# A fixed, woven instruction order with one-bank PSUM tiles in an attention, Fourier and FFN kernel

## The chip, the core and the metric

The kernel runs on one core of a Trainium2 chip. The metric is the device time in microseconds (us), as the median of several timed executions. The span that a profile shows is that of one profiled execution, 1 to 3 us shorter than the timed ones. Five engines matter: TensorE (PE; PEld is its weight load), VectorE (DVE), ScalarE (ACT), GpSimd (POOL) and SyncE (SP; SPq is its queue, which issues most transfers).

## The reference

For each of 8 batches, 512 rows of `x` attend to a 32-row state, and the state attends to the rows, in 8 heads of 64. The 544 rows that come out go through a real Fourier mix over rows and columns, a normalisation and a two-layer FFN. Cut to what matters:

```python
scores = x @ state.T / 8;  xread = softmax(scores) @ state     # 512 rows of each head
scores2 = state @ x.T / 8; sread = softmax(scores2) @ x        # 32 rows of each head
x = concat([xread, sread])                  # (8, 544, 512) after the heads are joined
u = x + real(fft(fft(x, axis=1), axis=2))
un = (u - mean(u)) / sqrt(var(u) + 1e-6)
out = u + relu(un @ w_ch1) @ w_ch2          # 512 -> 2048 -> 512
```

## The kernel before

One function, `front(b)`, does attention and transform of a batch; `ffn` does the two layers. The order of instructions on each engine was left to a scheduler. Every PSUM tile outside of the FFN is a pair of banks, of which there are two buffers.

```python
psQ = ctx.enter_context(tc.tile_pool(name="psQ", bufs=2, space=bass.MemoryType.PSUM))
psF = ctx.enter_context(tc.tile_pool(name="psF", bufs=2, space=bass.MemoryType.PSUM))
# ... x of batch 0, then the weights, which share the DMA engines with it
load_x(0)
for q in range(4):
    nc.gpsimd.dma_start(out=w1[:, :, q * 512:(q + 1) * 512], in_=w1v[:, :, q * 512:(q + 1) * 512])
# ... cut: w2, state, sine and cosine tables
def q2(name, dt=F32):
    return psQ.tile([128, 2, 512 if dt == F32 else 1024], dt, name=name, tag="q")
# ... in front(b): the state's reads (srp), copied into row block 0 of XR head by head
srp = q2("srp")
for g in range(2):
    for si in range(4):
        nc.tensor.matmul(srp[:, g, 0:257], lhsT=E[:, si, g, :], rhs=xin[:, si, 257 * g:257 * g + 257], ...)
rcs = wk.tile([128, 2], F32, name="rcs", tag="rcs")
nc.vector.reciprocal(rcs, srp.rearrange("p g c -> p (g c)")[:, 0:769:768])
# ... for g in 2, hh in 4: eight small rows, all on VectorE
nc.vector.tensor_scalar(XR[0:32, 0, c0:c0 - 64:-1], in0=srp[ph, g, ...], scalar1=rcs[ph, g:g + 1], ...)
# ... in ffn, for each of the four output tiles of a batch
nc.vector.scalar_tensor_tensor(ot, in0=po, scalar=rstd, in1=u, op0=ALU.mult, op1=ALU.add)
for d in dst:
    if isinstance(d[0], slice):                      # straight rows, and the "low" rows: 1 or 31 rows each
        nc.sync.dma_start(out=d[1], in_=ot[d[0], :])
        continue
    b, k = d                                         # reversed rows: out to DRAM, and from there to their place
    nc.sync.dma_start(out=r_dram[b, k], in_=ot)
    nc.sync.dma_start(out=out[b, top:top - 128:-1, :].rearrange("r (c n) -> c r n", c=2),
                      in_=r_dram[b, k].rearrange("r (c n) -> c r n", c=2))
# ... the main loop
ready = [front(0)]
for b in range(B):
    ready.append(front(b + 1))                       # while it exists
    ffn(*ready[b])
    if b % 4 == 3:
        ffn(*front_low(b // 4))
```

The softmax here doesn't subtract the row's maximum and nothing guards it: scores larger than these inputs give would overflow.

Of the kernel before, what the change touches and what calls it, by code (L numbers as in the profile page):

```python
# [12 lines left out]
F32 = mybir.dt.float32  # L13
BF16 = mybir.dt.bfloat16
# [14 lines left out]
def kernel(  # L29
# [24 lines left out]
    psQ = ctx.enter_context(tc.tile_pool(name="psQ", bufs=2, space=bass.MemoryType.PSUM))  # L54
    psF = ctx.enter_context(tc.tile_pool(name="psF", bufs=2, space=bass.MemoryType.PSUM))

# [7 lines left out]
    li = singles.tile([128, dm], I32, name="li")  # L64
    lt = singles.tile([128, NM], I32, name="lt")
    nc.gpsimd.iota(pi_[:, 0:2], pattern=[[128, 2]], base=1, channel_multiplier=1)
    nc.gpsimd.iota(pi_[:, 3:5], pattern=[[128, 2]], base=0, channel_multiplier=1)
    for hh in range(4):
# [10 lines left out]
    nc.sync.dma_start(  # L79
        out=stf.rearrange("p b g d -> p (b g) d"),  # L80
        in_=state.rearrange("b (g hh) j d -> (hh j) (b g) d", hh=4),
    )
    xin_bufs = []
    for i in range(2):
        t = singles.tile([128, 4, 514], BF16, name=f"xin{i}")
        xin_bufs.append(t)

    def load_x(b):
        xs = wk.tile([128, 4, dm], F32, name="xs", tag="xs")
        xb = x[b].rearrange("h s d -> s h d")  # L90
        for ps, si, rows in (
            (slice(0, 128), 0, xb[1:129]),
            (slice(0, 128), 1, xb[129:257]),
            (slice(0, 128), 2, xb[256:384]),
            (slice(0, 128), 3, xb[384:512]),
            (slice(0, 1), 2, xb[0:1]),
        ):
            nc.sync.dma_start(out=xs[ps, si, :].rearrange("p (h d) -> p h d", d=D), in_=rows)
        t = xin_bufs[b % 2]
        if b == 0:  # L100
            for si in range(4):
                if si % 2 == 0:
                    nc.vector.tensor_copy(t[:, si, 1:513], xs[:, si, :])  # L103
                else:
                    nc.scalar.copy(t[:, si, 1:513], xs[:, si, :])
        else:
            nc.gpsimd.tensor_copy(t[:, :, 1:513], xs)  # L107

    for i in range(2):
        nc.vector.memset(xin_bufs[i][:, :, 0:514:513], 1.0)  # L110
    load_x(0)
# [4 lines left out]
    for q in range(4):  # L116
        nc.gpsimd.dma_start(out=w1[:, :, q * 512:(q + 1) * 512], in_=w1v[:, :, q * 512:(q + 1) * 512])
    for q in range(2):
        nc.gpsimd.dma_start(out=w2[:, q * 8:(q + 1) * 8, :], in_=w2v[:, q * 8:(q + 1) * 8, :])


    stb = singles.tile([128, B, 2, 264], BF16, name="stb")
    nc.vector.memset(stb.rearrange("p b g c -> p (b g c)").bitcast(F32), 0.0)
    for hh in range(4):
        pq = slice(32 * hh, 32 * hh + 32)
        nc.vector.memset(stb[pq, :, :, hh:hh + 1], 1.0)
        nc.vector.memset(stb[pq, :, :, 260 + hh:261 + hh], 1.0)
        nc.scalar.copy(stb[pq, 0, :, 4 + 64 * hh:68 + 64 * hh], stf[pq, 0, :, :])
    for hh in range(4):
        pq = slice(32 * hh, 32 * hh + 32)  # L130
        nc.scalar.copy(stb[pq, 1:, :, 4 + 64 * hh:68 + 64 * hh], stf[pq, 1:, :, :])
# [11 lines left out]
    gen1 = wk.tile([128, 4096], F32, name="gen1", tag="hT")  # L143
    gen2 = wk.tile([128, 4096], F32, name="gen2", tag="hT")
# [22 lines left out]
    f, q = turn(NM, Stot, l1, [0, 1, 2], gen1)  # L167
    w = 2.0 * PI / Stot * shrink
    nc.scalar.activation(CT, q[:, 0:2, :], AF.Sin, bias=halfpi, scale=-w)
    nc.scalar.activation(ST, f[:, 0:2, :], AF.Sin, bias=0.0, scale=w)  # L170
    for hh in range(4):
        pq = slice(32 * hh, 32 * hh + 32)
        nc.scalar.activation(CL[pq, hh, :], q[pq, 2, :], AF.Sin, bias=halfpi[pq], scale=-w)
        nc.scalar.activation(SL[pq, hh, :], f[pq, 2, :], AF.Sin, bias=0.0, scale=w)
    f, q = turn(dm, dm, l2, [3, 4], gen2)
    w = 2.0 * PI / dm * shrink
    nc.scalar.activation(T2[:, 0:2, :], q, AF.Sin, bias=halfpi, scale=-w)
    nc.scalar.activation(T2[:, 2:4, :], f, AF.Sin, bias=0.0, scale=-w)
    alt = T2[0:1, 2, :].rearrange("p (n two) -> p two n", two=2)
    nc.vector.memset(alt[:, 0, :], 1.0)  # L180
    nc.vector.memset(alt[:, 1, :], -1.0)
# [17 lines left out]
    def q2(name, dt=F32):  # L199
        return psQ.tile([128, 2, 512 if dt == F32 else 1024], dt, name=name, tag="q")  # L200

    def stats_of(u, name):
# [4 lines left out]
        rstd = wk.tile([128, 1], F32, name="rstd", tag=name, bufs=12)  # L207
# [4 lines left out]
    def front(b):  # L212
# [5 lines left out]
        G = wk.tile([128, 4, NM], BF16, name="G", tag="G")  # L218
        sb = stb[:, b, :, :]


        sTp = q2("sTp", BF16)
        for pr in range(4):
            g, hp = pr // 2, pr % 2
            nc.tensor.transpose(sTp[:, 0, pr * 128:(pr + 1) * 128], sb[:, g, 4 + 128 * hp:132 + 128 * hp], ident)
        sT = wk.tile([128, 4, 128], BF16, name="sT", tag="sT")
        nc.vector.tensor_copy(sT, sTp[:, 0, 0:512].rearrange("p (a b) -> p a b", b=128))
        xTp = q2("xTp", BF16)
        xT = wk.tile([128, 4, S], BF16, name="xT", tag="xT")
        for pr in range(4):  # L230
            g, hp = pr // 2, pr % 2
            for si in range(4):
                o = (pr % 2) * 512 + si * 128
                nc.tensor.transpose(xTp[:, g, o:o + 128], xin[:, si, 1 + 128 * pr:129 + 128 * pr], ident)  # L234
        nc.vector.tensor_copy(xT[:, 0:2, :], xTp[:, 0, :].rearrange("p (a b) -> p a b", b=S))  # L235
        nc.scalar.copy(xT[:, 2:4, :], xTp[:, 1, :].rearrange("p (a b) -> p a b", b=S))  # L236


        eTp = q2("eTp")
        for g in range(2):  # L240
            for lo, hi, src in ((0, NM, slice(0, NM)), (NM, S, slice(S - 1, NM - 1, -1))):
                for hp in range(2):
                    nc.tensor.matmul(eTp[:, g, lo:hi], lhsT=sT[:, 2 * g + hp, :], rhs=xT[:, 2 * g + hp, src],
                                     start=(hp == 0), stop=(hp == 1))
        ET = wk.tile([128, 2, S], BF16, name="ET", tag="ET")
        nc.scalar.activation(ET, eTp, AF.Exp, scale=scale)  # L246


        esp = q2("esp")
        for si in range(4):  # L250
            for pr in range(4):
                hp = pr % 2
                o = (si % 2) * 256 + pr * 64
                nc.tensor.matmul(
                    esp[:, si // 2, o:o + 64].rearrange("p (h j) -> p h j", j=Ns),
                    lhsT=xT[:, pr, si * 128:(si + 1) * 128],
                    rhs=sT[:, pr, 64 * hp:64 * hp + 64].rearrange("p (h j) -> p h j", j=Ns)[:, :, ::-1],
                    start=True, stop=True)
        E = wk.tile([128, 4, 2, 128], BF16, name="E", tag="E")
        nc.scalar.activation(E.rearrange("p a b c -> p (a b c)"), esp.rearrange("p a b -> p (a b)"), AF.Exp, scale=scale)  # L260


        srp = q2("srp")
        for g in range(2):
            for si in range(4):
                nc.tensor.matmul(srp[:, g, 0:257], lhsT=E[:, si, g, :], rhs=xin[:, si, 257 * g:257 * g + 257],  # L266
                                 start=(si == 0), stop=(si == 3))
        rcs = wk.tile([128, 2], F32, name="rcs", tag="rcs")
        nc.vector.reciprocal(rcs, srp.rearrange("p g c -> p (g c)")[:, 0:769:768])  # L269


        def xread(c0, rev, name):
            p = q2(name)
# [4 lines left out]
            return p  # L278

        def normalise(p, o, ps=slice(0, 128)):  # L280
# [10 lines left out]
        for k in range(2):  # L291
            p = xread(128 * k, False, "xfp")
            normalise(p, XF[:, k, 0:512])
            p = xread(256 + 128 * k, True, "xrp")
            normalise(p, XR[:, k, 1:513])
            if k == 0:
                for g in range(2):
                    for hh in range(4):
                        c0 = 512 - (256 * g + 64 * hh)
                        ph = slice(32 * hh, 32 * hh + 32)  # L300
                        nc.vector.tensor_scalar(  # L301
                            XR[0:32, 0, c0:c0 - 64:-1], in0=srp[ph, g, 1 - g + 64 * hh:65 - g + 64 * hh],
                            scalar1=rcs[ph, g:g + 1], scalar2=None, op0=ALU.mult)
        p = xread(256 - 32 * bq, False, "xlp")
        normalise(p, XL[pq, 0:512], pq)


        Sm = wk.tile([128, 2, 514], BF16, name="Sm", tag="Sm")
        nc.vector.tensor_add(Sm, XF, XR)  # L309
# [115 lines left out]
    for b in range(B):  # L425
        if b + 1 < B:
            if b + 2 < B:
                load_x(b + 2)
# [34 lines left out]
```

## Time and profile before

| | before |
|---|---|
| time, median of 3 | 467.31 us (467.19 to 467.83) |
| span of the profile | 466.0 us |
| head: start to the first FFN matmul | 75.0 us |
| middle: to the end of the last matmul | 371.4 us |
| tail: to the end of the span | 19.6 us |

The division into head, middle and tail carries the whole argument. In the head TensorE waits for data, in the middle it should be full, and in the tail only transfers are left. The busy times of the engines, before, from the page's first part (us, share of the span, instructions):

```profile
PE 348.8 (75%) x2008; PEld 175.3 (38%) x2008; DVE 204.3 (44%) x472; ACT 134.2 (29%) x221; POOL 58.7 (13%) x139
```

TensorE is the busiest, but it lacks a quarter of the span. A busy TensorE also ran at half clock here (the granted clock was 0.50 from 380 to 385 us), so the prediction counts pitches, the distance from one start to the next, and not this busy time. The other lines of before stand in the prediction.

### The profile page before, as it was taken

Reading aid. Unit: us, or ns where it says so; the run is one execution under the profiler, and the core shown is the slowest. Engines: PE = TensorE matmul, PEld = TensorE weight load, DVE = VectorE, ACT = ScalarE, POOL = GpSimd, SP = SyncE. Lnnn points to the kernel's source line nnn. Section 1 sums busy time; section 2 is a strip of 40 time slices with the busy share of each in tenths; the row PEclk is TensorE's granted clock in tenths of the full one; section 3 lists DMA queues with packets and bytes.
Section 4 is the critical chain, followed back from the end, with each engine's and each line's share of the span. In section 5 each row is a group of like instructions: output and inputs, shape, how many; then the busy total and the mean of one; then the engine's idle time right before and its main releaser. Section 6 shows DMA issues by size and latency. Waiting matters only on the chain. (4 is left out here: it accounts for less than half of the span.)

```text
span 466.0 us, 5169 instructions
## 1 busy us (share of the span) xinstructions
PE 348.8 (75%) x2008; PEld 175.3 (38%) x2008; DVE 204.3 (44%) x472; ACT 134.2 (29%) x221; POOL 58.7 (13%) x139
## 2 busy tenths in 40 slices
PE   1013458999999998997883999989778944979830
PEld 0012125445545443553371444445333521434510
DVE  6630743772662916284427451136532165141210
ACT  5049024331444230443150252501233201430200
POOL 9001211120111201101100021000120001000000
PEclk9999988999999999999987899999989977889985
DMA  9998600402100121201100200035100000002020
GB/s 172 196 208 166 116 1 1 92 23 91 39 8 0 46 75 61 76 16 46 46 2 0 96 35 6 0 102 139 61 17 32 37 1 0 0 23 108 31 88 22
DMA packets 48695, 26.55 MB, mean 57 GB/s; under 512 B 36128, under 2 KB 44320, under 8 KB 48672
## 3 DMA queue, kind: packets, MB, share of 16 engines
q1 hardware_dynamic: 44480, 22.04, 17.9%
q0 software_dynamic: 4192, 4.19, 5.4%
q8 instruction: 15, 0.25, 0.2%
q14 instruction: 8, 0.07, 0.0%
HBM read 21.51 MB, written 13.11 MB: 74 GB/s over the span
## 5 line engine op out<-in xcount | busy, mean ns | idle before, releaser
L408 PE MATMUL po<-w,hT 128*128 128x512 bf16 x544 | 126.2, 381 | 5.4 <-DVE ot L411 5.4
L399 PE MATMUL ph<-unT,w 128*128 128x512 bf16 x512 | 123.5, 384 | 0.2
L404 ACT ACTIVATE hT<-ph 128x512 bf16<-128x512 f32 (+1 forms) x120 | 63.2, 534 | 92.2 <-PE ph L399 81.9
L399 PEld LDWEIGHTS <-w 128*128 128x128 bf16 x640 | 59.7, 101 | 59.6 <-issue 10.5
L408 PEld LDWEIGHTS <-hT 128*128 128x128 bf16 x544 | 53.0, 98 | 65.2 <-issue 7.6
L402 DVE TENSOR_SCALAR hT<-ph 128x512 bf16<-128x512 f32 (+1 forms) x40 | 24.2, 605 | 81.9 <-PE ph L399 75.2
L411 DVE SCALAR_TENSOR_TENSOR ot<-po,rstd,U 128x512 f32<-128x512 f32 x32 | 23.2, 744 | 39.8 <-PE po L408 34.4
L360 ACT COPY unT<-tp 128x512 bf16<-128x512 bf16 x32 | 17.8, 587 | 67.2 <-PE tp L358 67.0
L358 PE MATMUL tp<-ident,ub 128*128 128x128 bf16 x128 | 13.5, 238 | 21.5 <-DVE ub L355 21.3
L234 PE MATMUL xTp<-ident,xin 128*128 128x128 bf16 x128 | 12.0, 248 | 22.5 <-DVE xin L103 20.6
L346 DVE TENSOR_TENSOR U<-yp,XF 128x512 f32<-128x512 f32 x16 | 11.1, 691 | 27.4 <-PE yp L344 27.2
L325 ACT CAST G<-gep 128x576 bf16<-128x576 f32 x8 | 5.1, 638 | 61.7 <-PE gep L323 61.7
L107 POOL CAST xin<-xs 128x2048 bf16<-128x2048 f32 x7 | 13.2, 1893 | 73.7 <-DMA xs<-in_x_dram 41.6
L344 PE MATMUL yp<-T,G 128*128 128x512 bf16 x64 | 21.0, 441 | 0.9 <-ACT unT L360 0.8
L209 POOL TENSOR_TENSOR rstd<-rstd,mhalf 128x1 f32<-128x1 f32 x34 | 20.9, 616 | 2.7
L358 PEld LDWEIGHTS <-ub 128*128 128x128 bf16 x128 | 8.3, 104 | 33.0 <-DVE ub L355 32.5
L204 DVE BATCH_NORM_STATS2 st<-U 128x6 f32<-128x512 f32 x32 | 20.4, 681 | 0.0
L312 POOL COPY XN<-Sm 128x2 bf16<-128x2 bf16 x8 | 2.0, 247 | 144.4 <-DVE Sm L309 144.4
L236 ACT COPY xT<-xTp 128x1024 bf16<-128x1024 bf16 x8 | 8.1, 1009 | 41.4 <-DVE xT L235 41.4
L269 DVE RECIPROCAL rcs<-srp 128x2 f32<-128x2 f32 x8 | 1.4, 171 | 41.7 <-PE srp L266 41.7
L208 POOL TENSOR_TENSOR rstd<-mv,epst 128x1 f32<-128x1 f32 x34 | 6.7, 196 | 99.3 <-DVE mv L206 98.8
L234 PEld LDWEIGHTS <-xin 128*128 128x128 bf16 x128 | 9.9, 114 | 23.6 <-DVE xin L103 20.8
(113 smaller groups left out, 343.7 us busy)
## 6 DMA issues: line engine op xcount, KB each, us to landing
xs<-in_x_dram SPq DMA_DIRECT2D x32, 256.0 KB
r_dram<-ot SPq DMA_DIRECT2D x16, 256.0 KB
out_dram<-r_dram SPq DMA_DIRECT2D x16, 256.0 KB
out_dram<-ot SPq DMA_DIRECT2D x16, 256.0 KB
w<-in_moe_w_ch_dram POOLq DMA_DIRECT2D x4, 512.0 KB, 11.8
w<-in_moe_w_ch_dram POOLq DMA_DIRECT2D x2, 1024.0 KB, 24.6
stf<-in_state_dram SPq DMA_DIRECT2D x1, 512.0 KB
out_dram<-ot SPq DMA_DIRECT2D x8, 62.0 KB
```

Of the source, the lines that this page charges most:

```text
L107: nc.gpsimd.tensor_copy(t[:, :, 1:513], xs)
L204: nc.vector.bn_stats(st6, u)
L209: nc.gpsimd.tensor_tensor(rstd, rstd, mhalf, op=ALU.pow)
L234: nc.tensor.transpose(xTp[:, g, o:o + 128], xin[:, si, 1 + 128 * pr:129 + 128 * pr], ident)
L344: nc.tensor.matmul(yp[:, 0, :], lhsT=G[:, c, 128 * k:128 * k + 128], rhs=T2[:, c, :], start=(c == 0), stop=(c == 3))
L358: nc.tensor.transpose(tp[:, 0, 128 * j:128 * j + 128], ub[:, 128 * j:128 * j + 128], ident)
L360: nc.scalar.copy(unT[:, :, col:col + 128], tp[:, 0, 0:512].rearrange("p (a b) -> p a b", b=128))
L399: nc.tensor.matmul(ph[:, :n], lhsT=w1[:, c, f * 128:(f + 1) * 128], rhs=unT[:, c, :], start=(c == 0), stop=(c == DC - 1))
L402: nc.vector.tensor_scalar_max(hT[:, f, :n], ph[:, :n], 0.0)
L404: nc.scalar.activation(hT[:, f, :n], ph[:, :n], AF.Relu)
L408: nc.tensor.matmul(po, lhsT=hT[:, f, i * 128:(i + 1) * 128], rhs=w2[:, f, :], start=(f == 0), stop=(f == FC - 1))
L411: nc.vector.scalar_tensor_tensor(ot, in0=po, scalar=rstd, in1=u, op0=ALU.mult, op1=ALU.add)
```

## The change

Its intent is to keep TensorE full by giving it, in one fixed order, small pieces of four batches in turn: layer 1 of batch b, layer 2 of b-1, transform of b+1, attention of b+2. The paired PSUM tiles become single banks where they can, so that three rotate. Only the reads of x and of the state keep one paired tile, `psX`. Beside that, relu goes to ScalarE, half of the eight state rows too, and x is loaded ahead of the weights. The core of the diff:

```diff
-    psQ = ctx.enter_context(tc.tile_pool(name="psQ", bufs=2, space=bass.MemoryType.PSUM))
+    psX = ctx.enter_context(tc.tile_pool(name="psX", bufs=1, space=bass.MemoryType.PSUM))
+    psQ = ctx.enter_context(tc.tile_pool(name="psQ", bufs=3, space=bass.MemoryType.PSUM))
+    ctx.enter_context(tc.manual_schedule(engines={ET_.PE, ET_.DVE, ET_.Activation, ET_.Pool, ET_.SP}))
 ... (weights: the loads come after a small GpSimd copy out of x of batch 0)
+    nc.gpsimd.tensor_copy(gate, xs_of[0][:, :, 0])
+    def qt(name, dt=F32):
+        return psQ.tile([128, 512 if dt == F32 else 1024], dt, name=name, tag="q")
+    def x2(name):
+        return psX.tile([128, 2, 512], F32, name=name, tag="x")
 ... (state reads)
+            p = x2("srp")
+            nc.vector.reciprocal(rcs, p.rearrange("p g c -> p (g c)")[:, 0:769:768])
+                    if g == 0:
+                        nc.vector.tensor_scalar(o, in0=i, scalar1=rcs[ph, g:g + 1], scalar2=None, op0=ALU.mult)
+                    else:
+                        nc.scalar.activation(o, i, AF.Copy, scale=rcs[ph, g:g + 1])
 ... (layer 1: all relus on ScalarE; layer 2: one buffer of po, in the last step alternating with psQ)
+    weave((transform(0), 0, 1), (attend(1), 0, 1))
+    for b in range(B + 1):
+        streams.append((layer1(b), 0, 1))
+        low = layer2(("L", b // 4 - 1)) if b in (4, 8) else []
+        streams.append((low + layer2(b - 1, last=(b == B)), 0, 1))
+        streams.append((transform(b + 1), 0.04, 0.97))
+        streams.append(([lambda: cast_x(b + 2)], -0.1, -0.1))
+        streams.append((attend(b + 2), 0, 0.95))
+        streams.append(([lambda: load_x(b + 3)], 0, 0.1))
+        if b in (3, 7):
+            streams.append((low_rows(b // 4), 0.05, 0.5))
+            streams.append((layer1(("L", b // 4)), 0.55, 1))
+        weave(*streams)
```

`weave` sorts the pieces of all streams by their place between the two given fractions of a step. (The conditions on b are cut here.)

## The prediction

> **What bounds the kernel now.** I read the page's slices first, then its groups, the waits of TensorE, the timeline of TensorE and VectorE at the gaps, and last the end of the sync queue.
>
> In the slices (11.65 us each) TensorE does next to nothing for five slices, is nearly full for a long middle, and has holes in slices 21, 29, 33 to 36 and at the end. Where it has holes its granted clock falls too.
> ```profile
> PE   1013458999999998997883999989778944979830
> PEclk9999988999999999999987899999989977889985
> ```
> The groups and waits say what TensorE does and what it waits for.
> ```profile
> L408 PE MATMUL po<-w,hT 128*128 128x512 bf16 x544 | 126.2, 381 | 5.4 <-DVE ot L411 5.4
> L399 PE MATMUL ph<-unT,w 128*128 128x512 bf16 x512 | 123.5, 384 | 0.2
> ...
> PE tp L358 <- DVE ub L355: 21.3, 8, 3.3
> PE xTp L234 <- DVE xin L103: 20.6, 1, 20.6
> ```
> The 381 ns are a latency, not a pitch. In the timeline, in a dense stretch, 39 matmuls of the second layer start at 104.27 and the transposes behind them at 112.69: 8.42/39 = 0.216 us each.
> ```profile
> 104.27 8.58 PE L408 MATMUL po<-w,hT 128*128 128x512 bf16 x39
> 112.69 0.39 PE L225 MATMUL sTp<-ident,stb 128*128 128x128 bf16 x4
> ```
> Read so, the timeline gives these pitches: 0.122 us at 288 columns, 0.11 at 224 to 260, 0.057 for a 128-column transpose, 0.029 for the 64-column scores. TensorE's work at full clock: 1056 layer matmuls 228.6 us; 72 of the transform over d 15.6; 120 over s 14.8; state reads, scores and x reads (64, 64, 128, 80) 7.1 + 7.0 + 3.7 + 8.9; 296 transposes 16.8; 128 low-row matmuls 7.3. Sum: 310 us. I treat it as the floor of the middle, not of the whole.
>
> The remaining 156 us lie in three places.
>
> *Head, 75 us.* The first FFN matmul starts at 75.0; by then only front(0) and the 20 transposes of batch 1 (together 10 us of pitch) are done. x of batch 0 arrives in pieces (casts at 6.4, 9.7, 23.9, 30.8) because 8.4 MB of weights start at 3.1 and share the DMA engines.
>
> *Middle.* From 75 to the last matmul's end at 446.4, 371 us hold 300 us of work. The five-us windows show 45 us of idle; lower clock and small gaps are the rest. The idle is a front that runs alone: at 375 VectorE works and TensorE stands, and then TensorE goes on at half clock.
> ```profile
> 375.00:380.00 5.00, 0.99 (x6) 0.25 (x4) 4.71 (x15) 0.00 (x0) 0.00 (x0) 0.93 0.00 0
> 380.00:385.00 5.00, 3.84 (x16) 2.37 (x17) 1.90 (x5) 0.66 (x2) 0.55 (x2) 0.50 0.01 3
> ```
> (Columns: PE, PEld, DVE, ACT, POOL busy, clock, DMA share, GB/s.) The same happens near 217, 250, 336, 396 and 415.
>
> *Tail, 19 us.* The last result is in SBUF at 447.2; the span ends at 466.0. The sync queue issues ten stores until 455.0, and then a single one of 16 engines (share 0.07) carries the four 62 KB low-row stores at 26 GB/s.
> ```profile
> 442.75 12.24 SPq L414 DMA_DIRECT2D out_dram<-ot  x10
> 455.00:457.00 2.00, 0.00 (x0) 0.00 (x0) 0.00 (x0) 0.00 (x0) 0.00 (x0) 0.50 0.07 26
> ```
> VectorE (204 us) and ScalarE (134 us) have room on average.
>
> [...] in the trace a 288-element cast takes 4.32 us (7.95 to 12.27) while GpSimd clears tables until 12.1, against 0.42 us for a larger one after it. That counts in the new head.
>
> **The change part by part.**
>
> *Work of the engines.* TensorE's matmuls stay the same in number and size. VectorE loses 32 relus of 0.684 us (21.9), 8 small ones (2.3) and 32 of 64 state-read rows at 0.28 (9.0). ScalarE gains 32 relus at 0.60 (19.2) and the 32 rows (about 9), and pays one more start for each halved exp and G copy. Per batch I get about 20 us on VectorE and 18 on ScalarE, beside 36.7 on TensorE: neither becomes the bound on average.
>
> *Head.* x of batch 0 goes alone: 1.05 MB at the 174 to 196 GB/s seen in the windows is about 6 us, landed by 9. VectorE, in fixed order, first does the angle arithmetic: from about 5.8 (after GpSimd's clearing) 10 us of rows seen before, then four casts: 17.3. Attention(0) alone is a chain of transposes, two copies, four exps (ScalarE free at about 19 after the sine tables), then seven uses of the one paired PSUM tile, each some 0.5 us of cold matmul and 0.95 us of VectorE, and a fold of 1.7: done at 34. ScalarE's state blocks and casts of batch 1 (4 x 0.94 + 4 x 0.62) run from 28 to 34.5. Transform(0) beside attention(1) is bound by VectorE: 17 us of its work after a slow start of some 4 us, so layer 1 of batch 0 starts at 53. The weights, held back behind x and GpSimd's in-order list, are issued from about 20 and land by 50; layer 1 takes them quarter by quarter.
>
> *Middle.* Behind 53, TensorE has 310 less two attentions (4.45 each) and one transform (4.5): 296.5 us. By step: 22.8; five of 36.7; low rows 8.3; 32.2; 32.5; 17.3. In a full step VectorE is idle at first and 85% busy in the last 60%, where the transform's statistics and the x reads meet. I went through one step by hand in its fixed order: waits of 0.2 us at the single paired tile twice or so and at the single `po` (eviction about 1 us, some 1.4 us of other matmuls meanwhile) make 1 to 1.5 us. The dense stretch from 80 to 180 of before holds 94.6 us of pitch in 100 us; I take 96.5%, slightly better. 296.5/0.965 = 307. Step 0 has 17 us of VectorE work and the fold's leftover against 22.8 us of matmul; 3 us more. Last matmul: 53 + 307 + 3 = 363.
>
> *Tail.* The low rows now go first in the last step, 14 us before the last result, so their slow stores overlap it in part. But the sync queue still takes about 0.9 us for each of eight, the single engine 9.8 us for them, and the reversed rows still go out and back through DRAM behind them. I take 10 us, against 19.6 after the last matmul before: span 373. The timed runs are 1.3 us over the span (467.31 against 466.0): 374; rounded to 375.
>
> In savings: layer 1 starts 22 us earlier (75 - 53) with 13.4 us of work behind it instead of 10, which is 25; waits and slow clock in the middle fall from 71 to 13.5, which is 58; tail 9.6. Together 92 of 466.
>
> **The rivals.**
>
> *VectorE in fixed order becomes the bound in the late part of each step.* For: the scheduler of before could let whatever was ready go first, and now a wait at the head of any queue holds everything behind it, with one `po` and one paired tile. If each tile change costs 2 us (4 of `po`, 6 of the pair, of which half exposed), a full step is 43 instead of 38: 40 us more, 410. Against: VectorE's average load falls to about 55%, and the steps are two to three us apart.
>
> *The head is not shorter.* GpSimd reaches the weight issues only after the copies of the sine tables, and a late layer-1 weight would hold TensorE at 60 or more. 8.4 MB took until about 35 from a start at 3 beside x; from 20 it could be 52. That costs up to 8 us: 383.
>
> [...]
>
> *Better than that:* if the head comes out at 48 and the tail at 5, 363.
>
> **Range and chances.** Head 53 +- 5, waits of the middle 13 +- 10, tail 10 +- 4; the errors more likely upward, as a fixed order has more ways to wait than I followed. Range 360 to 397. Even the first two rivals together stay under 430, so slower needs something that I don't see.
>
> **What would show it.** The first `ph` matmul at 50 to 58, with weights landed; TensorE full from there, clock 1.00 in nearly all slices; waits of `po` on `ot` and of x reads on XR and XF short and many instead of the 3.3 us ones on `ub`; VectorE's busy time down to 170 to 175, ScalarE's up to about 165; last matmul at 358 to 370 and some 10 us of stores after it. Wrong would be: five-us windows in mid-step with TensorE under 4.5; a clock below 1; a long wait at the start of layer 1 for weights or `unT`; a tail of 15 or more.

53 of head, 307 and 3 make 363 at the last matmul, with 10 of tail 373 of span, 374 timed, rounded to 375.

Measured numbers for what it says without one:

- The 288-element cast of 4.32 us beside GpSimd's clearing takes 0.31 us in before_gate (below), where it starts at 7.93 and the clearing is over by 7.2.
- x of batch 0 beside the weights: its casts start at 6.4, 9.7, 23.9 and 30.8; in before_gate, where x goes first, at 6.3, 9.6, 12.2 and 15.5.
- "Cold matmul": the two 260-column matmuls of an x read take 0.61 to 0.64 us at 47 to 50 us of the kernel before, and 0.38 at 119. The granted clock in the window from 47 to 50 is 1.00; what made them slow is not shown.
- "One more start": an exp of 1024 columns takes 1.02 us before, each of its two halves 0.60 after; a G copy of 576 columns takes 0.64, each half 0.40.
- A wait at the head of a queue: in before_gate a GpSimd cast waits 17.05 us for x, a small copy stands behind it, and TensorE waits 7.4 us for the copy.
- The clock in the hole near 379 us of the kernel before: its mean is 1.00 in the us before 379, 0.62 in the next and 0.50 in the one after. TensorE's longest idle stretch there until 379 is 2.0 us, with 0.40 us of work from 378 to 379.

## The result, and the profile after

The changed kernel took 403.91 us (403.43 to 404.0, four runs), against 467.57 us for the kernel before in the same rounds. The ratio is 0.863 (95% interval 0.8606 to 0.8653): faster by 13.7%. Ratios here are the mean time of one kernel's fast runs over that of the other's of the same rounds, so they are not quite the ratio of the medians. Executions over 1.5% slower than the fastest of the same kernel are left out of the means. All outputs are right. The direction was right; the time lies 7 us above the top of the range.

The same three stretches, measured and predicted:

| | before | predicted | after | over the prediction |
|---|---|---|---|---|
| head, to the first FFN matmul | 75.0 | 53 | 59.1 | +6.1 |
| middle, to the end of the last matmul | 371.4 | 310 | 323.6 | +13.6 |
| tail | 19.6 | 10 | 19.5 | +9.5 |
| span | 466.0 | 373 | 402.2 | +29.2 |

So the head gave 15.9 us, the middle 47.8 and the tail next to nothing. (The expectations below have 382.8 for the end of the last matmul and 19.4 for the tail; the views give 382.66 and 19.5.) These are the slices of the changed kernel's page (TensorE's busy tenths and its granted clock, in 40 slices of 10.05 us) and the busy times (the trace lacks the records of 37 of the 2008 matmuls):

```profile
PE 324.7 (81%) x1971; PEld 174.1 (43%) x2008; DVE 186.7 (46%) x426; ACT 162.7 (40%) x296; POOL 60.8 (15%) x134
...
PE   0245649769988998899899996999799999997900
...
PEclk9975758999999999999999999899999999999975
```

The deep holes of before in the last third are gone, and from the eighth slice on the clock is full or nearly so until the tail. What is left: six thin slices of head, with a clock of 0.5 to 0.7 in four of them; a 7 and a 6 in the eighth and ninth; 8s in the middle; a 6 at slice 25 and 7s at 29 and 37; and two empty slices at the end.

The waits of TensorE in the changed kernel (what waited, for what; us in total, times, longest):

```profile
PE xfp L300 <- ACT XR L329: 14.2, 8, 3.2
PE xTp L267 <- DVE xin L111: 11.4, 4, 10.9
PE po L500 <- DVE ot L505: 7.2, 7, 2.8
```

The wait of the transposes `tp` on `ub`, 21.3 us before, is gone entirely, as the change intended. In the first place is now the x read `xfp`, which waits eight times for ScalarE's last write of XR. Its counterpart before, where VectorE alone copied the state rows, was less than half of it:

```profile
PE xrp L277 <- DVE XR L301: 6.7, 8, 2.0
```

The timeline of the changed kernel shows what happens there (start, us, engine, line, operation, out<-in, count, and in brackets the idle time before it and what ended it):

```profile
239.71 0.15 DVE L319 RECIPROCAL rcs<-srp 128x2 f32<-128x2 f32 x1
...
239.90 0.27 DVE L327 TENSOR_SCALAR XR<-srp,rcs 32x64 bf16<-32x64 f32 x1
...
240.27 0.31 ACT L329 ACTIVATE XR<-srp,rcs 32x64 bf16<-32x64 f32 x1 [1.53 <-DVE XR L327]
...
240.61 0.28 DVE L327 TENSOR_SCALAR XR<-srp,rcs 32x64 bf16<-32x64 f32 x1 [0.43 <-ACT XR L329]
...
242.61 0.38 PE L300 MATMUL xfp<-stb,ET 128*128 128x260 bf16 x2 [0.81 <-ACT XR L329]
```

The eight rows of the state read do not run on the two engines side by side. ScalarE waits for VectorE's row, VectorE for ScalarE's, in turn. From the reciprocal at 239.71 to ScalarE's last row (start 242.25, 0.31 us long) it takes 2.85 us, and the next x read needs the tile that they all read. A little later in the same step TensorE waits for VectorE's other work. Windows of the changed kernel (columns as in the prediction: busy PE, PEld, DVE, ACT, POOL, clock, DMA share, GB/s):

```profile
240.00:245.00 5.00, 4.19 (x28) 2.19 (x27) 3.58 (x10) 2.93 (x8) 0.79 (x2) 1.00 0.09 31
245.00:250.00 5.00, 2.20 (x11) 0.99 (x11) 4.34 (x9) 1.16 (x2) 2.64 (x3) 1.00 0.00 0
```

In the second window TensorE works 2.20 us of 5 and VectorE 4.34. The prediction had named a five-us window under 4.5 in mid-step as a sign against it. The timeline of these five us says which row of VectorE is too long, and what waits behind it:

```profile
246.53 1.89 POOL L116 CAST xin<-xs 128x2048 bf16<-128x2048 f32 x1
...
247.17 1.40 DVE L333 TENSOR_TENSOR XE<-XL 32x256 bf16<-32x256 bf16 x1
...
249.67 1.02 PE L500 MATMUL po<-w,hT 128*128 128x512 bf16 x4 [2.75 <-DVE ot L505]
```

The add of 256 elements takes 1.40 us beside GpSimd's cast and 0.28 us without it (the mean is 1.14 us over the eight batches of this kernel, and 0.285 us in a version below where ScalarE does the cast). `po` has one buffer, so layer 2 stands until VectorE comes to it.

The end of the sync queue in the changed kernel (SPq issues; the bracket is missing, as the queue's waits are seen in the gaps between rows):

```profile
364.15 7.31 SPq L508 DMA_DIRECT2D out_dram<-ot  x9
373.12 0.69 SPq L512 DMA_DIRECT2D r_dram<-ot  x1
382.44 0.63 SPq L513 DMA_DIRECT2D out_dram<-r_dram  x1
383.16 1.87 SPq L508 DMA_DIRECT2D out_dram<-ot  x1
385.12 0.38 SPq L512 DMA_DIRECT2D r_dram<-ot  x1
391.84 0.61 SPq L513 DMA_DIRECT2D out_dram<-r_dram  x1
```

The first write of reversed rows to DRAM is issued at 373.12, and its trip to the output, which waits for it, at 382.44: 9.3 us for a 256 KB write. The second takes 6.7 us (385.12 to 391.84). In front of the first are the low rows' stores, in front of the second the first trip. With nothing slow in front such a write takes 2 us, as low_16 below shows. A window behind the first write shows what is slow: the DMA share of 0.06 is about one engine of 16 (16 x 0.06), and the low rows' stores are what is left to move.

```profile
380.00:381.00 1.00, 1.00 (x7) 0.41 (x6) 0.00 (x0) 0.00 (x0) 0.00 (x0) 1.00 0.06 25
382.26 1.41 DVE L505 SCALAR_TENSOR_TENSOR ot<-po,rstd,U 128x512 f32<-128x512 f32 x2 [5.72 <-DMA out_dram<-ot]
```

The second line is VectorE's: it sits idle for 5.72 us until a store frees one of the three `ot` buffers, and so the second reversed tile goes out late too.

### The profile page after: what moved, and what is told of

It is laid out like the page before. It is cut to its first block, busy times and chain, and to the rows that moved or that the text cites. A ratio compares the mean times of both kernels' runs of the same rounds, so it can differ in the third digit from the quotient of the medians.

```text
span 402.2 us, 5181 instructions
## 1 busy us (share of the span) xinstructions
PE 324.7 (81%) x1971; PEld 174.1 (43%) x2008; DVE 186.7 (46%) x426; ACT 162.7 (40%) x296; POOL 60.8 (15%) x134
## 4 chain that ended last, share of the span: by engine, by line
PE 55%; DVE 24%; POOL 4%; ACT 4%; issue 4%; DMA 3%; another core or an unknown queue 1%; SPq 1%; DVEq 0%; ACTq 0%; POOLq 0%
PE ph L482 22%; PE po L500 20%; DVE st L233 3%; PE gp L378 3%; DVE ub L402 3%; DMA out_dram<-ot 3%; DVE ot L505 2%; PE yp L391 2%; DVE XR L327 2%; ACT XR L329 2%; DVE XR L304 2%; PE eTp L276 2%; PE xTp L267 2%; DVE U L395 1%; DVE U L393 1%
## 5 line engine op out<-in xcount | busy, mean ns | idle before, releaser
L482 PE MATMUL ph<-unT,w 128*128 128x512 bf16 x491 | 131.0, 384 | 1.1 <-issue 0.2
L484 ACT ACTIVATE hT<-ph 128x512 bf16<-128x512 f32 x128 | 76.5, 597 | 98.0 <-PE ph L482 96.0
L505 DVE SCALAR_TENSOR_TENSOR ot<-po,rstd,U 128x512 f32<-128x512 f32 x32 | 23.9, 750 | 75.1 <-PE po L500 68.0
L393 DVE TENSOR_TENSOR U<-yp,XR 128x511 f32<-128x511 f32 x16 | 10.9, 682 | 47.7 <-PE yp L391 47.7
L300 PE MATMUL xfp<-stb,ET 128*128 128x260 bf16 x32 | 7.1, 307 | 20.6 <-ACT XR L329 14.2
L300 PEld LDWEIGHTS <-ET 128*128 128x128 bf16 x80 | 6.4, 100 | 35.7 <-issue 15.1
L383 ACT CAST G<-gp 128x288 bf16<-128x288 f32 x32 | 12.8, 399 | 21.0 <-PE gp L378 15.3
L329 ACT ACTIVATE XR<-srp,rcs 32x64 bf16<-32x64 f32 x32 | 9.9, 310 | 26.0 <-DVE XR L327 26.0
L402 DVE TENSOR_SCALAR ub<-U,mv 128x512 bf16<-128x512 f32 x32 | 16.4, 512 | 1.1
L391 PE MATMUL yp<-T,G 128*128 128x512 bf16 x61 | 16.3, 379 | 0.4 <-ACT E L292 0.2
L327 DVE TENSOR_SCALAR XR<-srp,rcs 32x64 bf16<-32x64 f32 x32 | 9.0, 281 | 9.9 <-ACT XR L329 9.6
```

What stands on the lines that cost most here:

```text
L327: nc.vector.tensor_scalar(o, in0=i, scalar1=rcs[ph, g:g + 1], scalar2=None, op0=ALU.mult)
L329: nc.scalar.activation(o, i, AF.Copy, scale=rcs[ph, g:g + 1])
L391: nc.tensor.matmul(yp, lhsT=G[:, c, 128 * k:128 * k + 128], rhs=T2[:, c, :], start=(c == 0), stop=(c == 3))
L402: nc.vector.tensor_scalar(t, in0=ud, scalar1=mv[:, 0:1], scalar2=None, op0=ALU.subtract)
L482: nc.tensor.matmul(ph[:, o:o + n], lhsT=w1[:, c, f * 128:(f + 1) * 128], rhs=un_of[key][:, c, :], start=(c == 0), stop=(c == DC - 1))
L484: nc.scalar.activation(hT[:, per * i:per * i + per, :].rearrange("p a b -> p (a b)"), ph, AF.Relu)
```

## The experiments

My theory after the result had four parts: the state rows' turns cost some 10 us; VectorE's crowded late part of each step costs some 10 more; the low rows' stores and the trips of the reversed rows, each on few engines (DMA shares of 0.06 and 0.14), make the tail; the fixed order itself is right. The rivals: the turns are harmless because something else would wait at the same place; the excess is simply the fixed order (a scheduler would do better); the tail is due to the last batch's arithmetic and order. The table gives the steps of the main loop in us, each from the first relu of a batch to that of the next. In the prediction a full step has 36.7 us of pitch.

| | first relu | 0 | 1 | 2 | 3 | 4 | 5 | 6 | last matmul ends | tail |
|---|---|---|---|---|---|---|---|---|---|---|
| after | 61.1 | 30.0 | 39.1 | 39.6 | 44.9 | 44.7 | 39.2 | 32.9 | 382.7 | 19.5 |
| rows_two | 58.3 | 28.6 | 37.8 | 38.4 | 43.7 | 43.3 | 38.0 | 32.9 | 372.2 | 18.9 |
| phase | 61.6 | 37.0 | 37.8 | 37.9 | 43.5 | 39.3 | 35.5 | 32.4 | 376.1 | 19.0 |
| both_mid | 57.5 | 34.7 | 36.8 | 36.8 | 43.4 | 39.1 | 34.5 | 32.4 | 366.3 | 19.1 |
| free_order | 60.5 | 24.7 | 39.6 | 40.3 | 69.9 | 39.1 | 39.3 | 33.2 | 401.0 | 29.7 |

(Steps 3 and 4 hold the low rows of the first four batches too. phase and both_mid move half an attention one step forward, so only their sums and their steps 1 and 2 compare with the others.)

### rows_two: the state reads in two tiles of one bank

```diff
-            p = x2("srp")
+            ps = [qt("srp0"), qt("srp1")]
-                    nc.tensor.matmul(p[:, g, 0:257], ...)
+                    nc.tensor.matmul(ps[g][:, 0:257], ...)
-            nc.vector.reciprocal(rcs, p.rearrange("p g c -> p (g c)")[:, 0:769:768])
+            nc.vector.reciprocal(rcs[:, 0:1], ps[0][:, 0:1])
+            nc.vector.reciprocal(rcs[:, 1:2], ps[1][:, 256:257])
-                    i = p[ph, g, 1 - g + 64 * hh:65 - g + 64 * hh]
+                    i = ps[g][ph, 1 - g + 64 * hh:65 - g + 64 * hh]
```

> The eight blocks of state-read rows go out of two one-bank tiles instead of one paired tile. Theory A (in the changed kernel VectorE and ScalarE take turns because both read one tile, so the eviction takes 2.9 us where I had counted 1.3): they run beside each other, eviction about 1.5 us, TensorE's wait on ScalarE's rows falls from 14.2 us to under 4, time down by 8 to 12 us to 392 to 396. Rival B (VectorE's load late in each step is what holds TensorE, the turns only fill a wait that is there anyway): the rows run side by side too, but the wait moves to other evictions and the time falls by less than 3 us.

393.16 us, ratio 0.8388 (0.8347 to 0.8429), against the 403.91 us and 0.863 of the changed kernel: 10.8 us less. The rows now run at once, four on each engine, in the timeline of this run:

```profile
232.03 1.17 DVE L328 TENSOR_SCALAR XR<-srp,rcs 32x64 bf16<-32x64 f32 x4
232.09 1.28 ACT L330 ACTIVATE XR<-srp,rcs 32x64 bf16<-32x64 f32 x4 [1.23 <-DVE rcs L320]
```

Both engines write into XR as before, and both work at once; so it was the common tile that they read, not the one they write, that made the turns. The trace also tells who asks for the turns: in the changed kernel every row after the first carries a semaphore wait for the other engine's row before it, and here only the first row of each engine carries a wait; the turns are in the program, and no run here tells whether the chip would need them. The wait of `xfp` on ScalarE's XR is gone from the list of waits. The edit does one thing more: the state reads leave the single buffer `psX` for the three of `psQ`, so the x reads need not wait for these rows at all. How much of the gain is this, and how much the end of the turns, was not told apart. 2.8 us of the gain lie before the first relu, 1.4 in step 0 and 1.2 to 1.4 in each of steps 1 to 5.

### rows_dve: all eight rows back on VectorE

```diff
-                    if g == 0:
-                        nc.vector.tensor_scalar(o, in0=i, ...)
-                    else:
-                        nc.scalar.activation(o, i, AF.Copy, scale=rcs[ph, g:g + 1])
+                    nc.vector.tensor_scalar(o, in0=i, scalar1=rcs[ph, g:g + 1], scalar2=None, op0=ALU.mult)
```

> All eight blocks back on VectorE, as before the change. Theory A: eviction 2.35 instead of 2.9 us and no hand-over; down by 2 to 5 us although VectorE gets 9 us more work. Rival B (VectorE's load is the bound late in the step): up by 3 to 8 us, since VectorE gets the 9 us just there.

400.25 us, ratio 0.8544 (0.8502 to 0.8586): faster than the shared rows by 3.7 us, though VectorE has more to do. The wait of `xfp` falls from 14.2 us to 9.6 us and now names VectorE. So the split onto ScalarE, which the prediction had booked as relief, cost more than it brought as long as the tile was shared. The split with two tiles, outside `psX`, is 7.1 us faster (400.25 to 393.16).

### phase: the x reads of attention in the early part of a step

```diff
-            streams.append(([lambda: cast_x(b + 2)], -0.1, -0.1))
-            streams.append((attend(b + 2), 0, 0.95))
+            streams.append((heads.pop(b + 2), 0, 0.42))        # pieces 7 on of attention b+2
-            streams.append(([lambda: load_x(b + 3)], 0, 0.1))
+            a = attend(b + 3); heads[b + 3] = a[7:]
+            streams.append(([lambda: cast_x(b + 3)], 0.44, 0.44))
+            streams.append((a[:7], 0.5, 0.97))                   # transposes, scores, exps
+        if b + 4 < B:
+            streams.append(([lambda: load_x(b + 4)], 0, 0.1))
```

(Step 0 does the whole of attention 2 and the first part of attention 3.)

> The attention of a batch is moved half a step: its evictions on VectorE lie in the first 42% of a step, the transform's statistics stay in the second half; nothing else changes. Rival B: full steps fall from 39 to 40 us to 37 to 38 and the holes at 75 to 90, 115 to 125, 155 to 165 and 240 to 250 close; down by 8 to 15 us. Theory A alone: the turns of VectorE and ScalarE stay 2.9 us, TensorE's wait on ScalarE's rows stays at 10 us or more; down by under 4 us.

396.53 us, ratio 0.8458 (0.8411 to 0.8504): 7.4 us less than the changed kernel. The waits of `po` on VectorE's eviction fall from 7.2 us to 2.6. In this run's list of TensorE's waits the state rows' turns stay:

```profile
PE xfp L300 <- ACT XR L329: 10.7, 6, 3.1
...
PE po L500 <- DVE ot L505: 2.6, 3, 0.9
```

So the place of the attention in the step is the second cost, and VectorE's crowding late in the step fits it. The edit also moves the x casts and loads by one step, and this is a rival: the 256-element adds no longer meet the casts, and all but one in the head are back at 0.28 us, some 1.1 us less for VectorE in each of steps 0 to 4. The trace of the changed kernel limits what that can be worth: in steps 1 and 2 TensorE's longer waits end at 123.1 and 162.6 us, just when the long adds begin (123.0 and 162.5), and of the 2.75 us at 249.67 the longer add explains 1.1. The casts alone were not moved in a run of the changed kernel.

### both_mid: both edits together

> The two cures of the middle together: state-read rows in two one-bank tiles (10.8 us by itself) and the attention moved half a step (7.4 us by itself). If they cure different waits they add up: 384 to 388. If both relieve the same late part of the step, as VectorE's load there would have it, the sum is 11 to 14 us: 390 to 393.

386.84 us, ratio 0.825 (0.8202 to 0.8297): 17.1 us less than the changed kernel, where the sum of the two alone is 18.1. So most of the two costs is separate. In the middle alone, by one profile of each, they give 7.7 and 7.1 us, and 12.8 together; some 2 us are common. Step 1 in the windows of the changed kernel and of this run, one after the other:

```profile
91.00:130.00 39.00, 36.65 (x226) 19.66 (x229) 20.92 (x49) 17.82 (x33) 5.56 (x10) 1.00 0.10 35
```

```profile
92.00:129.00 37.00, 36.74 (x227) 19.82 (x230) 19.70 (x47) 17.70 (x35) 5.32 (x10) 1.00 0.10 36
```

The same work, 36.7 us of TensorE, now fills the step, which is at the prediction's pitch of 36.7 us. From the first relu to the last matmul it is 308.8 us.

### tail: the low rows a step earlier

```diff
-            low = layer2(("L", b // 4 - 1)) if b in (4, 8) else []
+            low = layer2(("L", 0)) if b == 4 else []
+            if e:                                   # e: b == 7; low_rows at 0.05-0.25, layer1 at 0.28-0.5
+                streams.append((layer2(("L", 1), last=True, turn=1), 0.55, 0.8))
+        order = (0, 2, 1, 3) if last and not turn else range(n)
```

> The second group's low rows are finished in step 7 (their slow stores with it), and in the last step the two reversed tiles come first. Theory: the 19.4 us after the last matmul are a queue on one DMA engine (low rows, then two trips through DRAM one behind the other); they fall to 4 to 7 us, time down by 12 to 15 us, the last matmul stays within 2 us of 382.8. Rival: the end is the fixed cost of issuing and landing stores, and falls by under 4 us.

402.74 us, ratio 0.8595 (0.8554 to 0.8637): 1.2 us less, within the intervals of the changed kernel; the expectation missed. In this run's sync queue a trip of reversed rows, issued at 363.0, stood before the low rows' stores, and they went out only at 363.7 to 373.8 (364.2 to 371.5 in the changed kernel):

```profile
363.71 10.12 SPq L509 DMA_DIRECT2D out_dram<-ot  x9
374.23 0.35 SPq L513 DMA_DIRECT2D r_dram<-ot  x1
383.18 0.62 SPq L514 DMA_DIRECT2D out_dram<-r_dram  x1
```

The write at 374.23 again takes 9.0 us. VectorE meanwhile waited 9.10 us for a free `ot` buffer (5.72 in the changed kernel), as its results had not left. The rows were computed earlier, but their slow stores were in the queue at the same time as before, so the run does not test stores that leave early.

### bounce_c16: the trip in 16 pieces instead of 2

```diff
-                    out=out[b, top:top - 128:-1, :].rearrange("r (c n) -> c r n", c=2),
-                    in_=r_dram[b, k].rearrange("r (c n) -> c r n", c=2))
+                    out=out[b, top:top - 128:-1, :].rearrange("r (c n) -> c r n", c=16),
+                    in_=r_dram[b, k].rearrange("r (c n) -> c r n", c=16))
```

> The trip of the reversed rows from DRAM to DRAM in 16 column pieces instead of 2, so that the first dimension is 16. Theory [...]: the DMA share in a trip goes from 0.06 to much more, a trip no longer holds up what is queued behind it, the 19.4 us after the last matmul fall to 10 to 14, time down by 5 to 9. Rival [...] 15 to 30 us at the end, time up by 10 or more.

395.7 us, ratio 0.8442 (0.8402 to 0.8482): 8.2 us less; the tail falls from 19.5 to 10.0 us and no other step moves by more than 0.3 us. Where an expectation speaks of one engine for the trip, the trace says about two: in the window of the changed kernel in which only a trip runs, the mean busy share of the 16 engines is 0.14, which is 2.2 engines. In this run the trips in 16 pieces soon have other transfers beside them; in the half us in which the first trip starts, 1.3 us after its issue and 0.6 us after that of the next store, the share is 0.89. On how many engines such a trip runs by itself is not shown. The two windows, of the changed kernel and of this run:

```profile
396.00:398.00 2.00, 0.00 (x0) 0.00 (x0) 0.00 (x0) 0.00 (x0) 0.00 (x0) 0.50 0.14 49
```

```profile
384.50:385.00 0.50, 0.00 (x0) 0.00 (x0) 0.00 (x0) 0.00 (x0) 0.00 (x0) 1.00 0.89 141
```

The pieces are eight times smaller (128 bytes instead of 1 KB), and still the trip is faster: the second is issued at 387.92 and the span ends at 393.5, 5.6 us at most, against 8.4 us in the changed kernel (issued at 391.84, landed at 400.24). In the sync queue of this run the second write no longer waits for the first trip (2.9 us instead of 6.7, from 385.06 to 387.92), while the first write still waits 9.3 us, behind the low rows' stores:

```profile
373.89 0.70 SPq L512 DMA_DIRECT2D r_dram<-ot  x1
383.22 0.56 SPq L513 DMA_DIRECT2D out_dram<-r_dram  x1
...
385.06 0.38 SPq L512 DMA_DIRECT2D r_dram<-ot  x1
387.92 0.56 SPq L513 DMA_DIRECT2D out_dram<-r_dram  x1
```

### low_16: the low rows' stores in 16 and 15 rows

```diff
-                    nc.sync.dma_start(out=o, in_=ot[ps, :])
+                    n = ps.stop - ps.start
+                    for lo, hi in ((0, 1),) if n == 1 else ((0, 16), (16, n)):
+                        nc.sync.dma_start(out=o[lo:hi], in_=ot[ps.start + lo:ps.start + hi, :])
```

> Only the stores of the low rows are changed: each block of 31 rows goes out as 16 and 15. [...] the single engine has 60 rows instead of 124, its 10 us before the first trip through DRAM become 5, and the time falls by 4 to 6 us. Rival ([...] the split changes nothing): under 1.5 us.

396.62 us, ratio 0.8456 (0.8422 to 0.849): 7.3 us less; the tail is 11.9 us. The edit also splits the 128-row stores into 16 and 112 rows, so it is not quite one change. The expectation held the 15 rows to be as slow as the 31, which leaves 60 rows on one engine; that was the author's estimate, and 7.3 us is more than the 4 to 6 that it allowed. On how many engines the pieces ran is not shown. The sync queue of this run is the counterpart of the last one: the first write now takes 2.0 us, and the second, behind a trip in two pieces (about two engines by the share above), 4.7 (380.81 to 385.46):

```profile
373.97 0.35 SPq L514 DMA_DIRECT2D r_dram<-ot  x1
376.01 0.61 SPq L515 DMA_DIRECT2D out_dram<-r_dram  x1
```

Together the two runs show each delay belonging to the transfer named. Neither this edit nor the trip's gives the whole tail, because each leaves the other's slow transfer in the way.

### best_a and best_b: everything together, and the last step's order

best_a is both_mid with the edits of bounce_c16 and low_16. best_b changes in addition the order of the four output tiles in the last step, so that the two reversed ones come first, each pair in its own PSUM pool:

```diff
+                other = last and i in (2, 3)
+                po_of[i] = (psQ if other else psF).tile(...)
-        return [lambda i=i, q=q: step(i, q) for i in range(n) for q in range(4)]
+        return [lambda i=i, q=q: step(i, q) for i in ((0, 2, 1, 3) if last else range(n)) for q in range(4)]
```

> State-read rows in two tiles, attention half a step earlier, trips in 16 pieces, low rows in 16 and 15, together. The middle's cures gave 17 us and the trips 8: if tail and middle are separate, 375 to 380, with 6 to 9 us after the last matmul.

> As best_a, and in the last step the two reversed tiles come before the two straight ones, so that no trip through DRAM is left after the last matmul: 4 to 5 us after it instead of 6 to 9, time 2 to 4 us below best_a. Rival: the last straight store takes as long as the trip's end: within 1 us of best_a.

best_a took 373.32 us, ratio 0.796 (0.7933 to 0.7987), somewhat better than expected; best_b 372.36 us, ratio 0.7945 (0.7917 to 0.7973). Both have a tail of 4.8 us instead of 19.5. The order of the last tiles is worth 1.0 us by the medians, inside the intervals, and nothing in the tail: best_b's rival held. TensorE's slices of best_b's page, 9.25 us each, have only the head left:

```profile
PE   0165639868999999999999999999999999999894
```

In its sync queue the two writes of reversed rows are followed by their trips after 2.0 and 2.9 us, not 9.3 and 6.7.

### cast_act: the x casts from GpSimd to ScalarE

```diff
-            nc.gpsimd.tensor_copy(t[:, :, 1:513], xs)
+            for si in range(4):
+                nc.scalar.copy(t[:, si, 1:513], xs[:, si, :])
```

(on best_b, for batches 2 and up)

> As best_b, with the casts of x for batches 2 to 7 on ScalarE instead of GpSimd. Theory (a GpSimd cast of 1.89 us holds VectorE up, 1.40 us for an add of 0.28): the long adds go, layer 1 starts 1 to 3 us earlier than in best_b, full steps stay at 36.8, time 1 to 4 us lower. Rival (ScalarE, in fixed order, now makes TensorE wait in turn, 2.5 us more per step): no gain or up to 4 us more.

371.36 us, ratio 0.7934 (0.7878 to 0.7991): not to be told from best_b. The short adds on VectorE get faster, from 0.42 us on average to 0.285, but in best_b only one of the eight, in the head, was still long (1.40 us), since the moved attention had taken the others out of the casts' way. The first relu comes 0.5 us earlier, which is within the scatter of equal heads (58.0 us in best_b, 59.0 in best_a). So this run says little of what the casts cost in the changed kernel.

### free_order: the change without the fixed order

```diff
-    ctx.enter_context(tc.manual_schedule(engines={ET_.PE, ET_.DVE, ET_.Activation, ET_.Pool, ET_.SP}))
```

> The changed kernel without the fixed order: the scheduler may choose, tiles, weaving in the source and head remain. If the fixed order carries the gain in the middle: 420 to 450, with fronts that run alone again. Rival: one-bank tiles and the order of the source carry it, the scheduler follows the source: within 2% of 404.

433.83 us, ratio 0.9255 (0.9206 to 0.9305): 29.9 us more than the changed kernel. Ten of them are in the tail (29.7 us), and 19 around the low rows: step 3 takes 69.9 us, and 3 and 4 together 109.0 us against 89.6. The rest nearly cancels: step 0 is 5.3 us shorter, the time behind step 6 some 3 us longer. A window of this run in that step:

```profile
205.00:240.00 35.00, 24.19 (x142) 12.31 (x143) 15.25 (x40) 8.56 (x18) 3.25 (x9) 0.80 0.13 37
```

TensorE works 24 of 35 us at a clock of 0.80. From 216 to 228 the x reads of one attention run alone on it, with waits of 3.0, 1.0, 1.0 and 1.0 us between them, and no layer matmul lies between them. In the other full steps the scheduler does nearly as well as the fixed order (39.6, 40.3 and 39.3 us for 39.1, 39.6 and 39.2). So the rival, that the order is the excess, is refuted for the change as a whole; but the fixed order's gain over this scheduler is one bad stretch and a tail, not a little in each step.

### before_gate: the kernel before, with x ahead of the weights

```diff
+        nc.gpsimd.tensor_copy(w1[:, 0, q * 512:q * 512 + 4], xs0[:, :, 0])
         nc.gpsimd.dma_start(out=w1[:, :, q * 512:(q + 1) * 512], in_=w1v[:, :, q * 512:(q + 1) * 512])
```

(and likewise for w2: the load of a weight tile must wait for a small copy out of x)

> The kernel before, with nothing changed but that the weight loads wait for x of batch 0. If the head is short because x goes first, layer 1 starts at 50 to 57 instead of 75 and the time falls by 17 to 25 us to 443 to 450, the middle staying as it is. Rival: the head is bound by the chain of front(0) and weights are then late: under 8 us.

456.58 us, against 468.81 for the kernel before of the same rounds: ratio 0.9768 (0.9686 to 0.9851), which is unclear at 2%, but below one. The loading order alone gives some 12 us of the 64, between the expectation and its rival; the first relu comes at 64.6 instead of 76.9. It could have been more. TensorE waits 7.4 us once for a tiny GpSimd copy, which stands in GpSimd's list behind a cast that waits 17.05 us for x of a later batch (timeline of this run):

```profile
44.28 1.89 POOL L107 CAST xin<-xs 128x2048 bf16<-128x2048 f32 x1 [17.05 <-DMA xs<-in_x_dram]
46.12 0.19 POOL L315 COPY XN<-Sm 128x2 bf16<-128x2 bf16 x1
```

The change moves this copy to VectorE, and so does not have that wait.

## Why the prediction was wrong, point by point

The direction and the three places of the gain were right. The pitches held: with two waits taken away (both_mid) steps 1 and 2 take 36.8 us for 36.7 of pitch. That its whole middle then takes 310.8 us, for 310 predicted of which 296.5 are pitch, is no proof of the parts: the first steps and those with low rows still hold waits. The weights were not late, the clock was 1.00 in nearly the whole middle, the waits on `ub` went, and ScalarE's busy time came out at 162.7 us for about 165. The span was 29.2 us over, in three terms of the sum.

**The middle, 13.6 us over: "I went through one step by hand in its fixed order ... make 1 to 1.5 us."** This is the step that failed: the waits at the single paired tile, taken as 0.2 us "twice or so", and at the single `po`. The x read behind the state rows alone waited 14.2 us in 8 waits, 1.8 us each, and `po` 7.2 us in 7. At 36.7/0.965 = 38.0 us a full step and 8.3/0.965 for the low rows, the five full steps (207.5 us) were 8.7 us over together. Step 0 was 3.4 us over its 26.6 (22.8/0.965 + 3), and the 2.0 us from the first matmul to the first relu were not in the sum; the last steps were 0.9 us under their 85.0, and rounding of the sum makes 0.4. Working by hand, I let VectorE and ScalarE evict the state rows side by side (the prediction doesn't write this out; the expectation of rows_two has the 1.3 us that I counted). They take turns, 2.85 us from the reciprocal to the last row where two tiles take 1.5 (231.84 to 233.37 in rows_two), as both read one tile. rows_two, which gives each engine a tile of its own outside `psX`, takes 7.7 us from the middle and 2.8 from the head; this is shown, though not how it divides between the turns and the freed `psX`.

The other part is my own first rival, VectorE in the late part of a step. I had put it at 40 us if each tile change costs 2 us, and dropped it for the average load. (That sum was wrong in itself: half of ten changes at 2 us make 10 us a step, not the 5 in its 43.) phase shows 7.4 us for the place of the attention, 7.1 of them in the middle; that it is VectorE's load, and not in part the moved casts, is argued. The two edits together take 12.8 us from the middle (321.6 to 308.8 us after the first relu), nearly all of the 13.6. The size was right neither in the sum (about zero) nor in the rival.

**The tail, 9.5 us over: "I take 10 us".** I had named all its parts, the 9.8 us of the single engine among them, and then assumed that they overlap. What I missed is in the trace of the changed kernel. It shows 16 landings for the write of 373.12: 15 come from 375.29 to 376.02 and the last at 382.42, 0.02 us before the trip is issued; the last of the low rows' stores in front lands at 381.78. Of the 16 of the write of 385.12, 14 come from 387.19 to 387.34 and two at 391.73 and 391.77; the first trip, in front, lands at 390.44 and 390.49. So most of each write is in after 2.2 to 2.9 us, and a last part comes only after the slow transfer in front: 9.3 and 6.7 us instead of 2. That this part sits on the engines that still carry the slow transfer is the author's reading. The two trips, too, run at a DMA share of 0.13 and 0.14, about two engines each, one behind the other. bounce_c16, low_16 and both in best_a show it: from 19.5 us to 10.0, 11.9 and 4.8. The run named tail shows that it isn't the place of the low rows' arithmetic.

**The head, 6.1 us over: layer 1 at 59.1 instead of 53.** Some 3 us of it are the same state rows, in the first two attentions (2.8 in rows_two; profiles of equal heads differ by about 1 us). The slow clock there, 0.5 to 0.7 in the slices from 20 to 60 us (most pairs of x-read matmuls take 0.59 to 0.62 us there, against 0.38 at 242.61), makes TensorE's share of the chain longer than the hand count; no run tells it from the rest, so some 3 us stay open.

**VectorE's busy time** was 186.7 us for 170 to 175. 6.8 us of that are the eight short adds at 1.14 instead of 0.285 us; the rest was not sought. In the trace the add ends at 248.57, just after GpSimd's cast beside it (248.42). The prediction had a slow VectorE cast beside GpSimd's clearing (4.32 us), and I had charged this to the head only, while a cast of 1.89 us stands in the head and in each of steps 0 to 4.

The range failed because each of its parts was too narrow: 53 +- 5 for the head against 59.1, 13 +- 10 for the middle's waits against 27.1 (323.6 - 296.5), 10 +- 4 for the tail against 19.5. Even all three at their upper ends make only 391.5 us of span. The misses of middle and tail are of one kind: two users of one thing that had been taken to work side by side.

best_b reaches 372.36 us, close to the 375 that I had predicted for the change as it stood, though by chance and not by the same parts: its tail is 4.8 us and not 10, and its head is still longer than predicted.

## What to carry to other kernels

When work is split between two engines, try a tile of its own for each to read (10.8 us here); look in the timeline for a chain "A waits for B, B waits for A" right after such a split. Before any latency is called hidden at the end, follow the queue in order: a small transfer on about one or two engines (DMA shares of 0.06 and 0.14) held up a large one behind it here (9.3 and 6.7 us instead of 2), and with the trip in 16 pieces instead of 2 the second of these was 2.9 us. An engine at 46% average load can still be what the others wait for in a stretch of each step (4.34 of 5 us here): predict by stretches, and move its work to where it is idle.
